# Logit spectra stored by frequency: long reads, short writes, a copied wrap and three more weight tiles

## The chip, the core and the metric

The program runs on one core of a Trainium2 chip. The metric is device time in microseconds (us). Engines are TensorE (PE, with its weight loads PEld), VectorE (DVE), ScalarE (ACT), GpSimd (POOL) and SyncE (SP), which here issues nearly all DMAs.

## What is computed

A spectral layer with soft thresholding, followed by a soft mixture of experts over all 8 x 2496 tokens:

```
X  = rfft(x, axis=1)                       # x: 8 x 2496 x 256
Yr = shrink(Xr @ w_r - Xi @ w_i + b_r)     # shrink: sign(y) * max(|y| - 0.01, 0)
Yi = shrink(Xr @ w_i + Xi @ w_r + b_i)
y  = irfft(Yr + 1j * Yi)                   # tokens, 19968 x 256
logits = y @ phi                           # 32 slots: 8 experts x 4
d = softmax over tokens;  slot_input = d.T @ y
slot_out[e] = relu(slot_input[e] @ w1[e]) @ w2[e]
out = softmax over slots (logits) @ slot_out
```

## The kernel before

**Transforms.** 2496 is 39 x 64, so a transform is one of length 39 (20 frequencies k are kept, K1) and one of length 64 (n, N2), joined by a transposition through DRAM. The 39-point matmuls work on three residues at once: R = 3 blocks of 39 tokens (or of 2 x 20 frequencies, real and imaginary, Q1 = 120 rows), each with G = 22 columns. 3 x 22 is 66, so the third block has 20 columns of its own and the first two of the signal once more.

**The main loop.** 40 steps, five groups of four frequencies for each of 8 batches. A step loads `ap` from the DRAM tile `adr` (line 387), transforms it (`px`), applies the weights (`pk`, `py`), shrinks on DVE and POOL (`ut`, `rt`), multiplies by phi (`pq`; its result `p_sb` is the logits' spectrum) and transposes `rt` into tiles `T`. Beside it the next batch's x is transformed (`pa`, `ast`) and written to `adr`.

**The logits of a batch** come from `p_sb` by an inverse transform of 32 columns (function `c_stages`, lines 604 to 706; `last_chain` from line 924 for batch 7). This is the place of the change:

1. `pg`: the 64-point matmul with the constant `sinv`. ACT copies it to `g_sb` (128 x 20 x 32). The rows are ordered n first, then real or imaginary (c).
2. `gd`, a DRAM tile `[64, 40, 32]`: `g_sb` is written to it in rows of 20 x 32 numbers, 2,560 B (line 619). Batch 7 writes three parts, as its frequencies get ready (line 936): 12, 4 and 4 of the 20.
3. `gp` (120 x 22 x 32): read from `gd` with four loads (lines 622 to 633, and 939 to 950), two of 40x22x32, one of 40x20x32 and one of 40x2x32 for the wrapped columns of the third block. Every contiguous piece has 32 numbers, 128 B.
4. ACT casts `gp` into `chpL`, DVE subtracts to get the rest `clpL`, and three matmuls per half give `pL` with the constant `m2`; `L` holds the logits. Batches 6 and 7 multiply `gp` itself, without the split.
5. From `L` come the running maximum (`mx`, `pm`, `mall`, `pb`), the exponentials `ee`, their forward transform (`pe`, `ea`, DRAM tile `ed`, read back as `eb`, then `pd`, `dd`) and the slot sums `pr` from `dd` and `T`.

**The tail.** After batch 7's `pr` come the experts (`psl`, `hps`, `po`) with 32 weight tiles of 512 KB, then the combine: 78 blocks of `pq`, copied by ACT and DVE and stored as `out`.

**What sets the order.** Every operation is a step of a generator with a due time; a heap runs them in that order, and the numbers in the table `PLAN` are the due times (the unit is a quarter of a step; TB = 166 is the end of the main loop). Each engine works through its list in that order and stops at the first thing that is not ready; so does SP's list of DMA issues (the helper `sp`, line 234; matmuls are recorded at line 240, the other engines at line 177). `PLAN["T_"]["wl"]` lists the 32 weight loads: due time, and where the tile lies: `r`, `a`, `x` and `T` are buffers that the main loop no longer needs (`x` and `T` in two halves of 256 KB), `t` and `h` are pools opened late. Pool `t` (tag `tw`) has `PLAN["nw"][1]` buffers of 4 KB per partition, shared by five tiles `T` of batch 6, weights, and the combine's `ct` and `chl`.

Of the kernel before, what the change touches and what calls it, by code (L numbers as in the profile page):

```python
# [11 lines left out]
F32 = mybir.dt.float32  # L12
# [37 lines left out]
def _constants():  # L50
    n1 = np.arange(N1)
    k1 = np.arange(K1)
    a39 = 2 * np.pi * (np.outer(n1, k1) % N1) / N1
    c39, s39 = np.cos(a39), np.sin(a39)
    s39[:, 0] = 0.0
    a64 = 2 * np.pi * (np.outer(np.arange(N2), np.arange(N2)) % N2) / N2
    q = np.outer(np.arange(N2), np.arange(N2)) % N2
    c64, s64 = np.cos(a64), np.sin(a64)
    c64[(q == 16) | (q == 48)] = 0.0
    s64[(q == 0) | (q == 32)] = 0.0  # L60

# [26 lines left out]
    smov = smov.reshape(128, K1 + 1, 64)
    smov = np.concatenate([smov[:, : KG + 1], smov[:, :1], smov[:, KG + 1 :]], axis=1).reshape(128, -1)
    sinv = suni[np.arange(128).reshape(2, N2).T.reshape(-1)].T  # L90
    sgn = np.ones((2, N2, K1))
    sgn[1] = sig.T
    sgn = sgn.reshape(128, K1)
    dsc = sgn * wk[None, :]

    ident = np.eye(128)
    dmask = np.tile(np.eye(32), (4, 4))
    f1a = f1.reshape(P1, R, 2, NGRP, KG).transpose(0, 3, 2, 4, 1).reshape(P1, Q1)
    f1 = f1.reshape(P1, R, 2 * K1).transpose(0, 2, 1).reshape(P1, Q1)
# [40 lines left out]
    "to": 0.7,  # L140
    "ws": [-29, -28.9, -28.8, 2],
    "late": {'6': {'cms': [19.75, 19.71, 860.75, 862, 864, 865], 'pd': [20.36, 20.37], 'pr': [31.55, 31.6, 31.65, 31.7, 31.75], 'pL': [5.4, 5.8], 'pm': 6.875, 'pb': 7.325, 'pe': [8.75, 9.75], 'pg': [0.875, 1.275], 'fr': {'sinv': 0, 'm2': 0, 'f1': 0, 'suni': 0}}, '5': {'pg': [1.1, 1.8], 'pL': [4.95, 5.75], 'pm': 6.8, 'pb': 7.15, 'pe': [9.2, 9.9], 'pd': [13.8, 14.8], 'pr': [15.0, 17.25, 19.5, 21.75, 24.0]}, '4': {'pr': [18.4, 20.49, 24.49, 28.49, 32.49]}},
    "T_": {'wl': [[-45, 'r'], [-44, 'r'], [-43, 'r'], [-31.0, 't'], [-30.7, 't'], [-29.4, 't'], [-27.6, 't'], [-27.8, 't'], [-11, 'a'], [-10.3, 'a'], [-9.6, 'a'], [-7.5, 'x'], [-6.4, 'x'], [1.11, 'x'], [1.07, 'h'], [1.08, 'h'], [1.09, 'h'], [1.1, 'h'], [1.11, 'h'], [13.55, 'h'], [13.1, 'h'], [13.6, 'h'], [13.6, 'h'], [13.61, 't'], [13.61, 't'], [13.61, 't'], [13.61, 't'], [13.61, 't'], [13.7, 'T'], [13.7, 'T'], [13.7, 'T'], [13.7, 'T']], 'cl': 16, 'cp': 46.5, 'ct': 46.6, 'du': [[-4.5, 0], [-2.4, 0], [1.2, 0]], 'd1': [5, 2, 4, 0, 0, 0], 'cm': [19.9, 19.91, 19.92, 25, 25.1, 25.2], 'cm7': [18, 20, 22, 23, 25, 27], 'ye': 0.2, 'te': [[5.6, 0.2], [5.5, 0.4]], 'pg': [-7, -3.25, -0.35], 'yt': 0.5, 'wr': -30.6, 'tp': [0, 0.9, 1.05, 0.5], 'tt': [[-0.4, 0.5, 0.6, 0.7, 0.8], [12, 12.1, 12.2, 12.3, 12.4]], 'z': 13.55, 'th': [0.1, 0.12], 'tl': [0.2, 0.25]},
    "f1": [1.5, 2.15],
    "kw": [[-40, 9]],
    "ap1": 1.85,
    "f0": 0.2,
    "nw": [3, 10, 9],
    "te": 'A',
    "tp": [0.5, 1.0, 1.9, 1.8],  # L150
    "tt": [2, 2.5],
# [29 lines left out]
def fourier_soft_moe_kernel(ctx: ExitStack, tc: tile.TileContext, t: dict, out: bass.AP):  # L181
    nc = tc.nc
# [3 lines left out]
    dr = ctx.enter_context(tc.tile_pool(name="dr", bufs=2, space=bass.MemoryType.DRAM))  # L186
# [30 lines left out]
    V, A, P = (_InOrder(tc, e) for e in (nc.vector, nc.scalar, nc.gpsimd))  # L217
# [15 lines left out]
    def sp(**kw):  # L233
        tc.keep_in_program_order(nc.sync.dma_start(**kw))  # L234
# [68 lines left out]
    ident, sgn, suni, sinv, dsc, dmask = (cols[k] for k in ("ident", "sgn", "suni", "sinv", "dsc", "dmask"))  # L303
    f1, m2 = cols["f1"][:P1], cols["m2"][:Q1]
# [273 lines left out]
    def halves(n, t0, times, out, const, fr, src, evac):  # L578
# [13 lines left out]
        for h in range(2):  # L592
# [8 lines left out]
            yield t0 + times[h] + 0.25  # L601
            evac(h, out[1](ps))

    def c_stages(b):
        ct_ = "ps"
        K_ = dict(PLAN, **PLAN["late"].get(str(b), {}))
        t0 = 20 * b + 20 + LAG
        yield t0 + PLAN["c0"]
        p_sb = psb[b]
        g_sb = wtile([128, K1, S], F32, "g_sb", f"g_sb{b}")  # L610
# [4 lines left out]
            lambda h, ps: A.copy(out=g_sb[:, h * 10 : h * 10 + 10, :].rearrange("p k s -> p (k s)"), in_=ps),  # L615
        )
        yield t0 + K_["pg"][1] + 0.35
        gd = dr.tile([N2, 2 * K1, S], F32, tag="gd", name=f"gd{b}")
        sp(out=gd.rearrange("n (c k) s -> (n c) k s", c=2), in_=g_sb)
        yield t0 + K_["pg"][1] + 0.9  # L620
        gp = wtile([Q1, G, S], F32, "gp", f"gp{b}")
        for r in range(R):
            ge = 22 if r < 2 else 20
            p0 = r * 2 * K1
            sp(
                out=gp[p0 : p0 + 2 * K1, :ge, :],
                in_=gd[22 * r : 22 * r + ge].rearrange("g k s -> k g s"),
            )
            if ge < G:
                sp(  # L630
                    out=gp[p0 : p0 + 2 * K1, ge:, :],
                    in_=gd[22 * r : 22 * r + G - ge].rearrange("g k s -> k g s"),
                )
# [51 lines left out]
        for c in range(2):  # L685
# [6 lines left out]
                out=dd[:, h * 10 : h * 10 + 10, :],  # L692
# [105 lines left out]
    TB = 4 * ns + LAG  # L798
# [125 lines left out]
    def last_chain():  # L924
        b = B - 1
        for (k0, k1), tk in zip(((0, 12), (12, 16), (16, 20)), T_["pg"]):
            ks = slice(k0, k1)
            n = (k1 - k0) * S
            yield TB + tk
            if k0 == 0:  # L930
                g_sb = wtile([128, K1, S], F32, "g7", f"g_sb{b}")
                gd = dr.tile([N2, 2 * K1, S], F32, tag="gd", name=f"gd{b}")
            ps = psum("pf", f"pg{b}_{k0}")
            mm(out=ps[:, :n], lhsT=sinv, rhs=psb[b][:, ks, :], start=True, stop=True)
            A.copy(out=g_sb[:, ks, :].rearrange("p k s -> p (k s)"), in_=ps[:, :n])
# [3 lines left out]
        for r in range(R):
            ge = 22 if r < 2 else 20  # L940
            p0 = r * 2 * K1
            sp(
                out=gp[p0 : p0 + 2 * K1, :ge, :],
                in_=gd[22 * r : 22 * r + ge].rearrange("g k s -> k g s"),
            )
            if ge < G:
                sp(
                    out=gp[p0 : p0 + 2 * K1, ge:, :],
                    in_=gd[22 * r : 22 * r + G - ge].rearrange("g k s -> k g s"),
                )  # L950
# [310 lines left out]
```

## Time and profile before

| | |
|---|---|
| runs | 579.31, 576.2, 579.02 us; median 579.02 |
| profiled execution | 575.19 us, of it 573.4 us span, 1.8 us around it |
| granted TensorE clock over the span | 0.971 |
| TensorE busy | 528.8 us, 92% |
| DMA queue of SP | 116.73 MB, 73.0% of 16 engines' span |
| packets under 512 B | 46,802 of 92,884 |

A row of a timeline is start and duration in us, engine, line, operation, tiles as out<-in, shape, count, and in brackets how long the engine stood still before it and what ended that. Rows of the chain are start, us, what. "SPq L234 gp<-gd" is the issue on SP, "DMA gp<-gd" the transfer from its issue to the landing. A matmul's row can overlap the next one's, since they are pipelined. Rows of windows give for each engine the busy time and the number of instructions, then the granted clock (1.00 is full), the mean busy share of 16 DMA engines (overlapping packets can bring it over 1) and GB/s.

### The profile page before, as it was taken

The page shows a single profiled execution, that of the slowest core. Times are in us where ns is not written, and L with a number is a line of the kernel's source. Part 1 is how long each engine was busy: PE and PEld are TensorE (multiplying, and loading weights), DVE is VectorE, ACT ScalarE, POOL GpSimd, SP SyncE. Part 2 cuts the span into 40 slices and gives each one's busy share as a digit, 9 for nine tenths or more (in the row PEclk, how much of TensorE's full clock was granted, in tenths as well). Part 3 has the DMA queues.
Part 4 walks back from the last instruction along what each step waited for, and adds up shares of the span by engine and source line. Part 5 has one row for each costly group of instructions (what it writes and reads, how often), then busy time and mean ns, then how long its engine had stood idle before and what let it go on. Part 6 is the DMA issues. An engine that isn't in the chain of part 4 may idle for free.

```text
span 573.4 us, 11788 instructions
## 1 busy us (share of the span) xinstructions
PE 528.8 (92%) x4358; PEld 447.4 (78%) x4358; DVE 419.3 (73%) x837; ACT 298.6 (52%) x650; POOL 281.0 (49%) x258
## 2 busy tenths in 40 slices
PE   8668999999999999999999999998899989799894
PEld 4357999989898879889988888897687767367673
DVE  0254988789979897989689977986776764247783
ACT  4334555667566656665665656553333333037662
POOL 0035778667676666658655865773445412000100
PEclk9887999999999999999999999998989999999897
DMA  8779878667776858775787577866624489969898
GB/s 241 235 259 241 198 162 175 156 171 178 205 176 178 173 154 204 170 180 156 177 196 187 151 179 185 238 184 193 164 80 102 121 199 298 369 218 363 330 374 352
DMA packets 92884, 118.55 MB, mean 207 GB/s; under 512 B 46802, under 2 KB 68624, under 8 KB 92828
## 3 DMA queue, kind: packets, MB, share of 16 engines
q1 hardware_dynamic: 92572, 116.73, 73.0%
q10 hardware_dynamic: 256, 1.08, 0.5%
q8 instruction: 34, 0.56, 0.4%
q14 instruction: 22, 0.18, 0.1%
HBM read 68.42 MB, written 49.38 MB: 205 GB/s over the span
## 4 chain that ended last, share of the span: by engine, by line
PE 65%; DMA 14%; DVE 12%; ACT 3%; issue 2%; SPq 2%; POOL 0%; ACTq 0%; DVEq 0%; POOLq 0%
PE py L240 15%; PE px L240 10%; PE pq L240 8%; PE pk L240 7%; PE pa L240 7%; PE pt L530 4%; DMA gp<-gd 3%; DMA gd<-g_sb 3%; PE pr L240 3%; DMA ap<-adr 2%; SPq L234 2%; PE pc L1065 2%; DMA eb<-ed 2%; DMA xr<-in_x 2%; DVE mx L177 1%
## 5 line engine op out<-in xcount | busy, mean ns | idle before, releaser
L177 POOL TENSOR_TENSOR rt<-ut,rt 128x512 f32<-128x512 f32 x79 | 111.7, 1414 | 26.5 <-DVE rt L177 22.0
L177 POOL TENSOR_TENSOR xsl<-xsm,xsh 128x256 fp32r<-128x256 f32 x77 | 59.4, 772 | 107.3 <-DVE xsh L177 72.5
L177 POOL TENSOR_TENSOR xl<-xr,xh 117x512 fp32r<-117x512 f32 x73 | 98.4, 1349 | 21.8 <-ACT xh L177 13.8
L240 PE MATMUL px<-smov,ap 128*128 128x128 f32 x640 | 86.8, 280 | 5.7 <-DMA ap<-adr 3.9
L240 PEld LDWEIGHTS px<-smov,ap 128*128 128x128 f32 x640 | 81.5, 195 | 11.6 <-issue 4.7
L177 ACT COPY ast<-pa 120x512 f32<-120x512 f32 x86 | 50.6, 588 | 69.7 <-PE pa L240 68.1
L177 ACT CAST xth<-px 128x512 fp32r<-128x512 f32 x80 | 46.9, 586 | 74.0 <-PE py L240 38.2
L177 DVE SCALAR_TENSOR_TENSOR ut<-py,pk,k 128x256 f32<-128x256 f32 x160 | 69.5, 475 | 16.7 <-PE py L240 12.4
L177 DVE TENSOR_TENSOR xtl<-px,xth 128x512 fp32r<-128x512 f32 x80 | 54.6, 683 | 24.7 <-ACT xsm L177 22.6
L240 PE MATMUL py<-xth,nwsh 128*128 128x256 f32 x160 | 54.0, 337 | 0.0
L177 DVE TENSOR_SCALAR rt<-ut 128x512 f32<-128x512 f32 x69 | 53.3, 772 | 0.5
L240 PE MATMUL pk<-xsh,w_rh 128*128 128x256 f32 x160 | 49.3, 308 | 2.0 <-DVE xsh L177 2.0
L530 PE MATMUL pt<-pk,rt 128*128 128x128 f32 x320 | 45.9, 273 | 0.9 <-DVE dd L177 0.6
L177 ACT COPY T<-pt 128x512 f32<-128x512 f32 x70 | 42.0, 599 | 9.0 <-PE pt L530 7.0
L240 PE MATMUL pk<-xsl,w_rh 128*128 128x256 f32 x160 | 46.2, 289 | 0.0
L240 PE MATMUL pk<-xsh,w_rl 128*128 128x256 f32 x160 | 46.1, 288 | 0.0
L240 PE MATMUL py<-xtl,wdh 128*128 128x256 f32 x160 | 45.3, 283 | 0.0
L240 PE MATMUL py<-xth,wdl 128*128 128x256 f32 x160 | 45.2, 283 | 0.0
L240 PE MATMUL py<-xth,nwsl 128*128 128x256 f32 x160 | 45.2, 283 | 0.0
L240 PE MATMUL py<-xth,wdh 128*128 128x256 f32 x160 | 45.2, 282 | 0.0
L240 PE MATMUL py<-xtl,nwsh 128*128 128x256 f32 x160 | 45.1, 282 | 0.0
L240 PE MATMUL pq<-rhs,ct 128*128 128x512 f32 x156 | 43.1, 416 | 0.3 <-DVE ost L177 0.3
(186 smaller groups left out, 1245.8 us busy)
## 6 DMA issues: line engine op xcount, KB each, us to landing
ap<-adr SPq DMA_DIRECT2D x76, 256.0 KB
out<-ost SPq DMA_DIRECT2D x37, 512.0 KB
xr<-in_x SPq DMA_DIRECT2D x35, 480.0 KB
adr<-ast SPq DMA_DIRECT2D x20, 720.0 KB
w<-in_moe_w SPq DMA_DIRECT2D x25, 512.0 KB
adr<-ast SPq DMA_DIRECT2D x8, 480.0 KB
w<-in_moe_w SPq DMA_DIRECT2D x14, 256.0 KB
x<-in_x SPq DMA_DIRECT2D x11, 240.0 KB
```

Of the source, the lines that this page charges most:

```text
L177: return lambda *a, **k: self.tc.keep_in_program_order(f(*a, **k))
L234: tc.keep_in_program_order(nc.sync.dma_start(**kw))
L240: tc.keep_in_program_order(nc.tensor.matmul(**kw))
L530: tc.keep_in_program_order(nc.tensor.transpose(out=out, in_=in_, identity=identity))
L1065: nc.tensor.transpose(out=pc[:, i * P1 : (i + 1) * P1], in_=chls[b][x][:, 2 * (r + i) : 2 * (r + i) + 2].rearrange("p g h s -> p (g h s)") ...
```

## The change

`gd` is laid out by frequency, `[2, 20, 64, 32]`. A row of one c and k is now 64 x 32 numbers, 8 KB in one piece.

- **Write**: two DMAs, one for each c, from 64 partitions each. In DRAM every piece is 128 B. Batch 7 writes its three parts with six DMAs. `sinv` is no longer permuted, so that the partitions of `g_sb` are c first.
- **Read**: three DMAs of 40 rows, each a contiguous stretch of 22 x 32 numbers (2,816 B), or 20 x 32 (2,560 B) for the third block. That block now lies in partitions 0 to 39 of `gp`, and the rows of `m2` are permuted to match.
- **Wrap**: the third block's last two columns are copied by ACT from the first block of `gp` itself, 40x64 numbers. It stands just before the first cast of `gp` (in batches 6 and 7 ahead of ACT's copies of `pL`).

```
+    def gd_write(gd, g_sb, k0, k1):
+        for c in range(2):
+            sp(out=gd[c, k0:k1].rearrange("k n s -> n k s"), in_=g_sb[c * N2 : c * N2 + N2, k0:k1, :])
+
+    def gp_read(gp, gd):
+        rows = gd.rearrange("c k n s -> (c k) (n s)")
+        q = 2 * K1
+        for r in range(2):
+            sp(
+                out=gp[q + q * r : q + q * r + q].rearrange("p g s -> p (g s)"),
+                in_=rows[:, r * G * S : (r + 1) * G * S],
+            )
+        sp(out=gp[:q, : G - 2, :].rearrange("p g s -> p (g s)"), in_=rows[:, 2 * G * S :])
+
+    def gp_wrap(gp):
+        A.copy(out=gp[: 2 * K1, G - 2 :, :], in_=gp[: 2 * K1, :2, :])
...
-        gd = dr.tile([N2, 2 * K1, S], F32, tag="gd", name=f"gd{b}")
-        sp(out=gd.rearrange("n (c k) s -> (n c) k s", c=2), in_=g_sb)
+        gd = dr.tile([2, K1, N2, S], F32, tag="gd", name=f"gd{b}")
+        gd_write(gd, g_sb, 0, K1)
...
-        for r in range(R):
-            ge = 22 if r < 2 else 20
...
+        gp_read(gp, gd)
         L = wtile([P1, G, S], F32, "L", f"L{b}")
+        yield t0 + K_["pL"][0] - PLAN["cl"][0] - 0.01
+        gp_wrap(gp)
...
-    "nw": [3, 10, 9],
+    "nw": [3, 13, 9],
...
-    nc = _bacc.Bacc("TRN2", target_bir_lowering=False, num_devices=1)
+    nc = _bacc.Bacc("TRN2", target_bir_lowering=False, num_devices=1, dynamic_dma_scratch_size=1024)
```

The same three steps replace write and read in `last_chain`. The two constants change by one line each:

```
-    m2 = m2.reshape(Q1, P1)
+    m2 = m2[[2, 0, 1]].reshape(Q1, P1)
...
-    sinv = suni[np.arange(128).reshape(2, N2).T.reshape(-1)].T
+    sinv = suni.T
```

The build sets the DMA scratch to 1 KB per partition, and pool `t` has 13 buffers instead of 10. In the table of weight loads three `t` entries are new, at -24, -22 and -20 before TB. The two `x` entries at -7.5 and -6.4 move to 1.12 and 1.13 behind it. Of the late entries (13.55 and after), one more is `x`, and three that used `T` are gone.

On SP in batch 0, from the write of `gd` on (numbers in names are buffers), before:

```order
L234 DMA gd_1290<-g_sb_1178 128x640
L234 DMA ap_4_1315<-adr_182 64x4x256 x2
L234 DMA gp_1326<-gd_1290 40x22x32 x2
L234 DMA gp_1326<-gd_1290 40x20x32
L234 DMA gp_1326<-gd_1290 40x2x32
```

and now:

```order
L234 DMA gd_1290<-g_sb_1178 64x20x32 x2
L234 DMA ap_4_1316<-adr_182 64x4x256 x2
L234 DMA gp_1327<-gd_1290 40x704 x2
L234 DMA gp_1327<-gd_1290 40x640
```

The write became two issues, the read three, and `ap` still stands between them. So it is in batches 1 to 4; in batch 5 an `adr` write stands there, in batch 6 nothing, with a new weight load just ahead of the write.

On ACT in batch 0, at the cast of `gp`, before:

```order
L177 COPY ast_0_1395<-pa_0_1396 120x512
L177 CAST chpL_0_1405<-gp_1326 120x352
L177 CAST chpL_1_1421<-gp_1326 120x352
L177 CAST xth_4_0_1438<-px_4_0_1415 128x512
```

and now:

```order
L177 COPY ast_0_1395<-pa_0_1396 120x512
L177 COPY gp_1327<-gp_1327 40x64
L177 CAST chpL_0_1406<-gp_1327 120x352
L177 CAST chpL_1_1422<-gp_1327 120x352
L177 CAST xth_4_0_1439<-px_4_0_1416 128x512
```

The copy of the wrapped columns is new, ahead of both casts; the rest of ACT's list is the same, and so are the lists of the other compute engines but for the buffers that hold the weights.

On SP at the end of the main loop, batch 7's `gd` and `gp` and the weights `w` (tile number first) around them, before:

```order
L234 DMA w11_1_6426<-in_moe_w1 128x512
L234 DMA gd7_6432<-g_sb7_6431 128x384
L234 DMA w12_0_6439<-in_moe_w1 128x512
L234 DMA w12_1_6440<-in_moe_w1 128x512
L234 DMA gd7_6432<-g_sb7_6431 128x128 x2
L234 DMA gp7_6540<-gd7_6432 40x22x32 x2
L234 DMA gp7_6540<-gd7_6432 40x20x32
L234 DMA gp7_6540<-gd7_6432 40x2x32
L234 DMA w13_6547<-in_moe_w1 128x1024
...
L234 DMA ed7_6608<-ea7_6595 120x704
L234 DMA w19_6705<-in_moe_w2 128x1024
L234 DMA eb7_6707<-ed7_6608 64x20x32 x2
```

and now:

```order
L234 DMA gd7_6441<-g_sb7_6440 64x12x32 x2
L234 DMA gd7_6441<-g_sb7_6440 64x4x32 x4
L234 DMA gp7_6548<-gd7_6441 40x704 x2
L234 DMA gp7_6548<-gd7_6441 40x640
L234 DMA w14_6554<-in_moe_w1 128x1024
...
L234 DMA w20_1_6569<-in_moe_w2 128x512
L234 DMA ed7_6620<-ea7_6607 120x704
L234 DMA eb7_6717<-ed7_6620 64x20x32 x2
```

Weights w11 and w12 no longer stand between the writes. Between `gp` and `ed` there are now seven tiles (w14 to w20), before six (w13 to w18); the one between `ed` and `eb` is gone.

More of the change, by code (lines that the diff above doesn't have):

```diff
@@ L142 @@
     "late": {'6': {'cms': [19.75, 19.71, 860.75, 862, 864, 865], 'pd': [20.36, 20.37], 'pr': [31.55, 31.6, 31.65, 31.7, 31.75], 'pL': [5.4, 5.8], 'pm': 6.875, 'pb': 7.325, 'pe': [8.75, 9.75], 'pg': [0.875, 1.275], 'fr': {'sinv': 0, 'm2': 0, 'f1': 0, 'suni': 0}}, '5': {'pg': [1.1, 1.8], 'pL': [4.95, 5.75], 'pm': 6.8, 'pb': 7.15, 'pe': [9.2, 9.9], 'pd': [13.8, 14.8], 'pr': [15.0, 17.25, 19.5, 21.75, 24.0]}, '4': {'pr': [18.4, 20.49, 24.49, 28.49, 32.49]}},
-    "T_": {'wl': [[-45, 'r'], [-44, 'r'], [-43, 'r'], [-31.0, 't'], [-30.7, 't'], [-29.4, 't'], [-27.6, 't'], [-27.8, 't'], [-11, 'a'], [-10.3, 'a'], [-9.6, 'a'], [-7.5, 'x'], [-6.4, 'x'], [1.11, 'x'], [1.07, 'h'], [1.08, 'h'], [1.09, 'h'], [1.1, 'h'], [1.11, 'h'], [13.55, 'h'], [13.1, 'h'], [13.6, 'h'], [13.6, 'h'], [13.61, 't'], [13.61, 't'], [13.61, 't'], [13.61, 't'], [13.61, 't'], [13.7, 'T'], [13.7, 'T'], [13.7, 'T'], [13.7, 'T']], 'cl': 16, 'cp': 46.5, 'ct': 46.6, 'du': [[-4.5, 0], [-2.4, 0], [1.2, 0]], 'd1': [5, 2, 4, 0, 0, 0], 'cm': [19.9, 19.91, 19.92, 25, 25.1, 25.2], 'cm7': [18, 20, 22, 23, 25, 27], 'ye': 0.2, 'te': [[5.6, 0.2], [5.5, 0.4]], 'pg': [-7, -3.25, -0.35], 'yt': 0.5, 'wr': -30.6, 'tp': [0, 0.9, 1.05, 0.5], 'tt': [[-0.4, 0.5, 0.6, 0.7, 0.8], [12, 12.1, 12.2, 12.3, 12.4]], 'z': 13.55, 'th': [0.1, 0.12], 'tl': [0.2, 0.25]},
+    "T_": {'wl': [[-45, 'r'], [-44, 'r'], [-43, 'r'], [-31.0, 't'], [-30.7, 't'], [-29.4, 't'], [-27.8, 't'], [-27.6, 't'], [-24, 't'], [-22, 't'], [-20, 't'], [-11, 'a'], [-10.3, 'a'], [-9.6, 'a'], [1.07, 'h'], [1.08, 'h'], [1.09, 'h'], [1.1, 'h'], [1.11, 'h'], [1.12, 'x'], [1.13, 'x'], [13.55, 'x'], [13.6, 'h'], [13.6, 'h'], [13.6, 'h'], [13.6, 'h'], [13.61, 't'], [13.61, 't'], [13.61, 't'], [13.61, 't'], [13.61, 't'], [13.7, 'T']], 'cl': 16, 'cp': 46.5, 'ct': 46.6, 'du': [[-4.5, 0], [-2.4, 0], [1.2, 0]], 'd1': [5, 2, 4, 0, 0, 0], 'cm': [19.9, 19.91, 19.92, 25, 25.1, 25.2], 'cm7': [18, 20, 22, 23, 25, 27], 'ye': 0.2, 'te': [[5.6, 0.2], [5.5, 0.4]], 'pg': [-7, -3.25, -0.35], 'yt': 0.5, 'wr': -30.6, 'tp': [0, 0.9, 1.05, 0.5], 'tt': [[-0.4, 0.5, 0.6, 0.7, 0.8], [12, 12.1, 12.2, 12.3, 12.4]], 'z': 13.55, 'th': [0.1, 0.12], 'tl': [0.2, 0.25]},
     "f1": [1.5, 2.15],
@@ L617, in c_stages @@
         yield t0 + K_["pg"][1] + 0.35
-        gd = dr.tile([N2, 2 * K1, S], F32, tag="gd", name=f"gd{b}")
-        sp(out=gd.rearrange("n (c k) s -> (n c) k s", c=2), in_=g_sb)
+        gd = dr.tile([2, K1, N2, S], F32, tag="gd", name=f"gd{b}")
+        gd_write(gd, g_sb, 0, K1)
         yield t0 + K_["pg"][1] + 0.9
         gp = wtile([Q1, G, S], F32, "gp", f"gp{b}")
-        for r in range(R):
-            ge = 22 if r < 2 else 20
[L624 to L633, printed above, removed]
+        gp_read(gp, gd)
         L = wtile([P1, G, S], F32, "L", f"L{b}")
+        yield t0 + K_["pL"][0] - PLAN["cl"][0] - 0.01
+        gp_wrap(gp)
         yield from halves(
@@ L931, in last_chain @@
                 g_sb = wtile([128, K1, S], F32, "g7", f"g_sb{b}")
-                gd = dr.tile([N2, 2 * K1, S], F32, tag="gd", name=f"gd{b}")
+                gd = dr.tile([2, K1, N2, S], F32, tag="gd", name=f"gd{b}")
             ps = psum("pf", f"pg{b}_{k0}")
@@ L935, in last_chain @@
             A.copy(out=g_sb[:, ks, :].rearrange("p k s -> p (k s)"), in_=ps[:, :n])
-            sp(out=gd.rearrange("n (c k) s -> (n c) k s", c=2)[:, ks, :], in_=g_sb[:, ks, :])
+            gd_write(gd, g_sb, k0, k1)
         yield TB + 1
         gp = wtile([Q1, G, S], F32, "gp", f"gp{b}")
[L939 to L950, printed above, removed]
+        gp_read(gp, gd)
         L = wtile([P1, G, S], F32, "L", f"L{b}")
         mx = wtile([P1, 4, S], F32, "mx", f"mx{b}")
+        yield TB + 6.9
+        gp_wrap(gp)
         yield TB + 7
```

## The prediction, made before the result was known

> **What bounds the kernel now.** I read the page first: the busy shares and the chain that ended last.
>
> ```profile
> span 573.4 us, 11788 instructions
> PE 528.8 (92%) x4358; PEld 447.4 (78%) x4358; DVE 419.3 (73%) x837; ACT 298.6 (52%) x650; POOL 281.0 (49%) x258
> ...
> PE 65%; DMA 14%; DVE 12%; ACT 3%; issue 2%; SPq 2%; POOL 0%; ACTq 0%; DVEq 0%; POOLq 0%
> PE py L240 15%; PE px L240 10%; PE pq L240 8%; PE pk L240 7%; PE pa L240 7%; PE pt L530 4%; DMA gp<-gd 3%; DMA gd<-g_sb 3%; PE pr L240 3%; DMA ap<-adr 2%; SPq L234 2%; PE pc L1065 2%; DMA eb<-ed 2%; DMA xr<-in_x 2%; DVE mx L177 1%
> ```
>
> TensorE carries the program, but the edited transfer is on the chain with 6% of it (gd and gp), some 35 us. That is no gain yet: TensorE works beside most of it. What can be won is the time in which TensorE stands still behind it, so the second view is the waits of TensorE from 60 to 500 us (total us, times, longest).
>
> ```profile
> PE pd L240 <- DMA eb<-ed: 3.1, 1, 3.1
> PE pL L240 <- ACT chpL L177: 2.4, 1, 2.4
> PE pL L240 <- DMA gp<-gd: 2.4, 1, 2.4
> PE pm L648 <- DVE mx L177: 2.2, 5, 0.8
> PE px L240 <- DMA ap<-adr: 0.8, 2, 0.6
> ```
>
> Four places hang on gp. pL waits once for ACT's cast of gp (batch 5) and once for gp itself (batch 7). pm waits five times, in batches 0 to 4, for DVE, which had waited for the same cast. px waits in batch 6 for ap, whose loads stand behind gp's on SP. Everything below is the price of these four, and of eb in batch 7.
>
> **The transfer, priced.** In the chain, batch 5 (start, us, what):
>
> ```profile
> 380.90 2.24 DMA gd<-g_sb
> 383.15 0.29 SPq L234
> 383.49 2.12 SPq L234
> 385.66 4.34 DMA gp<-gd
> 390.10 0.49 ACT chpL L177
> ```
>
> Batch 7, where nothing is left to do beside it:
>
> ```profile
> 465.53 2.80 DMA gd<-g_sb
> 468.41 0.30 SPq L234
> 468.76 0.57 SPq L234
> 469.38 3.87 DMA gp<-gd
> 473.38 1.41 PE pL L240 x4
> ...
> 484.62 5.61 DMA eb<-ed
> ```
>
> Write and read are in series. From the first gp issue to the landing it takes 6.85 us in batch 5 (383.15 to 390.00) and 4.84 us in batch 7. The next view gives stretches by windows (PE, PEld, DVE, ACT, POOL busy, clock, DMA share, GB/s). In the first only gp's packets move, in the second eb's, in the third rows of 4 KB, in the fourth mostly gd's rows of 2,560 B.
>
> ```profile
> 469.50:472.00 2.50, 1.52 (x14) 1.28 (x12) 1.88 (x3) 1.36 (x3) 0.00 (x0) 1.00 0.80 124
> 485.50:487.00 1.50, 1.50 (x16) 1.50 (x15) 1.24 (x2) 0.93 (x3) 1.50 (x4) 1.00 1.14 183
> 474.00:478.00 4.00, 3.43 (x24) 2.80 (x23) 2.54 (x8) 0.90 (x2) 0.00 (x0) 1.00 1.00 383
> 437.00:438.00 1.00, 1.00 (x12) 1.00 (x11) 0.94 (x2) 0.23 (x1) 0.65 (x1) 1.00 0.73 278
> ```
>
> A 128 B piece costs 128 B / (124 GB/s / 16 / 0.80) = 13 ns of a DMA engine. gp's 2,640 pieces (338 KB) need 338/124 = 2.7 us. After the change the 128 B pieces are on the write: 2,560 of them, 64x20x32 per load, the same shape as eb's reads, which run at 183 GB/s, so 328/183 = 1.8 us. The old write needs 328/278 = 1.2 us. The new read is 120 rows of 2,560 or 2,816 B: 0.9 us at 383 GB/s, 2.7 us at worst as now; I take 1.3.
>
> The trace has no write of 128 B pieces. Bounds: 13 ns (as read) and 26 ns (each written as if read first); I take 13, since it is the row of the same size, and keep 26 as a rival.
>
> Now the issues, from SP's timeline (start, us, what, count):
>
> ```profile
> 412.50 1.24 SPq L234 DMA_DIRECT2D ap<-adr  x2
> ...
> 436.45 0.34 SPq L234 DMA_DIRECT2D gd<-g_sb  x1
> 439.78 2.67 SPq L234 DMA_DIRECT2D gp<-gd  x4
> 442.54 1.25 SPq L234 DMA_DIRECT2D ap<-adr  x2
> ...
> 463.38 0.89 SPq L234 DMA_DIRECT2D w<-in_moe_w  x2
> ...
> 468.41 2.85 SPq L234 DMA_DIRECT2D gp<-gd  x4
> 471.43 3.47 SPq L234 DMA_DIRECT2D w<-in_moe_w  x7
> ...
> 481.21 0.38 SPq L234 DMA_DIRECT2D w<-in_moe_w  x1
> 484.00 1.39 SPq L234 DMA_DIRECT2D eb<-ed  x2
> ```
>
> Four gp issues hold SP for 2.7 to 2.9 us. An issue of long rows takes 0.34 (gd), so three take about 1.0. Two gd issues take what eb's two take, 1.4 instead of 0.34, though the data of the first start meanwhile: I charge 0.3 to the path and 0.6 to the data (1.8 less 1.2), so **the write lands 0.9 us later** (bounds 0.3 and 2.7). Nearest to the new read is the 2.24 us in which gd's long rows landed in batch 5: third issue at 0.7, landing at 2.9 from the first issue, against 4.84. **The read lands 1.9 us sooner** (bounds 0.5 and 2.2).
>
> The copy of two columns on ACT: 40x64 elements. Its nearest row is 128 elements per partition:
>
> ```profile
> 470.23 0.29 ACT L177 COPY zrow<-dd 1x128 f32<-1x128 f32 x1
> ```
>
> I take 0.2 ahead of chpL in batches 0 to 5. It waits for the third load, as chpL behind it must anyway; queued behind both on ACT are the next xth and xsm, as now. In batch 7 only the second half of pL reads the copied columns, so it lies beside the first pL.
>
> **The four places.** *Batches 0 to 4*: the same three steps, here batch 0 in the chain:
>
> ```profile
> 107.23 3.98 DMA gd<-g_sb
> 112.45 3.77 DMA gp<-gd
> 117.32 1.60 DVE clpL L177
> ```
>
> The write shares the engines with the adr write ahead of it and ap follows it, so less comes off: 1.9 less 0.9 less 0.2 is 0.8 at best. Only the 2.2 us of pm's waits can be recovered, and DVE is crowded. I take 0.9 over the five (bounds 2.2 and -5.5, the second under the rival).
>
> *Batch 5*: gp's second issue stood 2.12 us behind the 720 KB adr write. Write +0.9, so gp starts at 384.0; the read takes 2.9 and some 1.1 of that queue; landing 388.0, copy 0.2, against chpL at 390.10: 1.9 earlier, of 2.4 waited; I take 1.7. TensorE's clock also fell after this wait:
>
> ```profile
> 390.60:392.60 2.00, 1.97 (x8) 1.88 (x9) 1.81 (x4) 1.75 (x5) 0.00 (x0) 0.50 1.06 294
> 392.60:394.60 2.00, 2.00 (x14) 1.98 (x14) 1.81 (x6) 0.45 (x1) 1.41 (x2) 0.76 0.22 86
> 473.40:476.00 2.60, 2.51 (x14) 1.89 (x15) 1.49 (x4) 0.90 (x2) 0.00 (x0) 1.00 1.00 362
> ```
>
> Granted 0.50 and 0.76 over 4 us cost 1.0 and 0.5 us of work; after the equal wait of batch 7 it stayed 1.00, so it is not certain to follow. With 0.6 us left of the wait I expect most of it back: 1.0. Sum 2.7 (bounds 0 and 3.9).
>
> [...]
>
> *Batch 6*: ap's loads stand behind gp's on SP; its issues end 1.7 us sooner and start up to 0.9 later, which removes the 0.6 us of px: 0.5. The copy waits for a load that is there by then.
>
> *Batch 7*: the three parts of the write are 64 KB at the end, so they grow little, and the four half tiles of weights (463.38 and the pair before) no longer stand ahead of them. I let the landing stay at 468.3 (1 us either way). The read: 468.3 + 2.9 = 471.2 against 473.25. TensorE has other work until 2.4 us before 473.38, so no more than that can come off; 2.2 (bounds 0.5 and 2.4).
>
> By the order on SP, shown with the change, no weight stands between the writes any more, nor between ed and eb. That tile (512 KB, 1.4 us at 383 GB/s) was ahead of eb, whose landing took 5.61 us. But seven tiles instead of six now stand ahead of ed; they start 2.2 us earlier, which is 840 KB at that rate, against 524 KB more. I take 0.4 (bounds -2.2 and 1.4). Batch 7: 2.6.
>
> **The rest is nothing.** The three further weight tiles load between the ap issue at 412.50 and gd at 436.45, behind ap and ahead of gd on SP: 1.6 MB in 24 us, hidden by the matmuls of two steps; a tile that ran into gd there would cost 1.4 us. After eb there are eleven tiles to load instead of twelve. The output phase is unchanged.
>
> **Sum**: 0.9 + 2.7 + 0.5 + 2.6 = 6.7 us. The profiled execution took 575.19 us (span 573.4), so it would take 568.5. It is the fastest seen: the three runs have a median of 579.02, and from that I predict 572.3.
>
> **Rivals.** *A, slower: the small pieces cost double when written.* Place: gd in batches 0 to 4. At 26 ns the write needs 1.8 us more, so chpL comes 1.0 to 1.1 us later than before (0.8 at best, less 1.8), five times, and pm's waits grow by it: +5.5. Batch 5 keeps nothing, batch 6 nothing, batch 7 2.2: +3.3, or 582.3. Between -6.7 at 13 ns and +3.3 at 26 ns it turns to a loss at about 22 ns a piece. For it: nothing in the trace writes so small. Against it: reads of this size show no surcharge. Chance 0.17. [...]
>
> *B, no change: another transfer ends last.* If ed must wait for the seventh tile (3.7 MB at 383 GB/s from 471.2 ends at 480.8, just where ed was issued), batch 7 gives nothing; if batch 5 keeps its slow clock, it gives 1.0. Left: 0.9 + 1.0 + 0.5 = 2.4, or 576.6. For it: the DMA share of 1.00 from 474 to 478. Against it: TensorE's 2.4 us wait for gp goes in any case. Chance 0.17.
>
> **How the numbers follow.** Forecast 0.66, B 0.17, A 0.17. About 0.5% (2.9 us) is what a measurement can tell from no change: faster 0.66; within it 0.20 (B and the mild part of A); slower 0.14. All best ends together are 10.5 us, so 568.5, and 1 us for the spread of runs gives 567.5; upward the range takes in B and the milder part of A, to 581.
>
> **What would show it.** Right: three gp issues of 0.3 us; gp landing some 3 us after the first; pL's two waits under 0.7 us; clock 1.00 at 390; chpL in batches 0 to 4 not later than before. Wrong: gd's landing over 2.5 us later, pm's waits growing, or eb landing no sooner in the program although pL does.

## The result, and the profile after

| | before | after |
|---|---|---|
| median, us | 577.61 (4 runs, 575.93 to 579.31) | 583.62 (4 runs, 580.85 to 585.09) |
| profiled execution, us | 575.19 | 583.56 |
| its span, us | 573.4 | 581.6 |

The ratio after to before is 1.0116, 95% interval 1.0068 to 1.0165: slower by 1.2%, some 6.7 us. The two medians are 6.0 us apart; every ratio here is of runs in the usual, faster state of the chip, the medians are of all runs. The forecast was 6.7 us faster, and the range ended at 581.0.

The page after, first its span, TensorE's row and the chain that ended last:

```profile
span 581.6 us, 11769 instructions
...
PE 531.1 (91%) x4358; PEld 448.1 (77%) x4358; DVE 413.8 (71%) x837; ACT 298.6 (51%) x658; POOL 279.5 (48%) x258
...
PE 67%; DMA 14%; DVE 8%; ACT 5%; SPq 2%; issue 2%; POOL 0%; ACTq 0%
PE py L240 15%; PE px L240 10%; PE pq L240 8%; PE pk L240 7%; PE pa L240 7%; DMA gd<-g_sb 4%; DMA gp<-gd 4%; PE pt L530 4%; PE pr L240 3%; SPq L234 2%; PE pc L1064 2%; PE pL L240 2%; DMA xr<-in_x 2%; PE pe L240 2%; DMA ap<-adr 1%
```

The same 4,358 matmuls take 531.1 us instead of 528.8; gd and gp moved up the chain, from 6% to 8% of it. TensorE's waits from 60 to 510 us (total us, times, longest):

```profile
PE pL L240 <- DMA gp<-gd: 4.8, 2, 2.7
PE pL L240 <- ACT chpL L177: 4.0, 2, 3.0
PE pd L240 <- DMA eb<-ed: 3.2, 1, 3.2
...
PE pm L656 <- ACT xth L177: 1.5, 3, 0.5
...
PE pm L656 <- DVE mx L177: 0.9, 2, 0.5
```

The wait of pL for gp and for its cast was to fall from 4.8 us (2.4 and 2.4) to under 1.4. It rose to 8.8. pm waits 2.4 us in all, as against 2.2 before, but now mostly for ACT. eb's wait, to shrink by 0.4, stayed (3.1 before, 3.2 now). SP's timeline shows where it comes from (start, us, what, count): the write of batch 5, an `adr` write behind it and the read, then batch 6 and batch 7.

```profile
385.87 1.42 SPq L234 DMA_DIRECT2D gd<-g_sb  x2
387.35 0.98 SPq L234 DMA_DIRECT2D adr<-ast  x1
391.21 1.12 SPq L234 DMA_DIRECT2D gp<-gd  x3
...
441.19 1.40 SPq L234 DMA_DIRECT2D gd<-g_sb  x2
446.68 1.06 SPq L234 DMA_DIRECT2D gp<-gd  x3
...
470.13 4.86 SPq L234 DMA_DIRECT2D gd<-g_sb  x6
477.00 1.05 SPq L234 DMA_DIRECT2D gp<-gd  x3
```

The read is issued when the write has landed. In batch 5 that is 5.34 us after the first gd issue (385.87 to 391.21; before 380.90 to 383.15, 2.25), in batch 6 5.49 us (before 436.45 to 439.78, 3.33). The write lands 3.1 and 2.2 us later, not 0.9. In batches 0 to 4, where it was slow before too (4.0 to 4.5 us), it lands 0.3 to 2.1 us later, in three of the five 0.84 to 0.87. In batch 7 six issues hold SP for 4.86 us. The three read issues do cost the 1.0 us that was forecast.

The chain in batch 5 (start, us, what):

```profile
386.51 4.65 DMA gd<-g_sb
...
392.00 3.57 DMA gp<-gd
...
395.74 0.49 ACT chpL L177
```

and in batch 7, with eb at its end:

```profile
472.43 0.57 SPq L234
473.05 0.62 SPq L234
473.71 0.61 SPq L234
474.37 2.58 DMA gd<-g_sb
...
477.73 3.46 DMA gp<-gd
...
492.86 5.50 DMA eb<-ed
```

From the last gp issue the read still takes 3.57 and 3.46 us, with long rows, where it took 4.34 and 3.87 with 2,640 pieces. From the first issue it is 4.19 us in batch 7 (477.00 to 481.19) against 4.84 before: 0.65 us saved, not 1.9. By the packets in the trace (2,816 and 2,560 B), its rows pass from 477.91 to 480.86; the last of them share the engines with a weight tile that SP issues right behind (rows of 4 KB, from 479.28 on).

Windows after (busy times, clock, DMA share, GB/s): the first two hold the write of batch 6, which has the DMA engines nearly to itself, the third gp's long rows, the fourth TensorE behind the wait of batch 5.

```profile
443.00:444.50 1.50, 1.50 (x16) 1.50 (x15) 1.05 (x3) 0.97 (x3) 1.05 (x1) 1.00 0.89 138
444.50:446.00 1.50, 1.50 (x15) 1.44 (x13) 0.88 (x3) 0.00 (x0) 0.73 (x1) 1.00 0.22 31
478.00:479.00 1.00, 0.58 (x6) 0.34 (x4) 0.82 (x2) 0.66 (x2) 0.00 (x0) 1.00 0.57 205
398.00:400.00 2.00, 2.00 (x8) 1.93 (x9) 1.97 (x7) 0.45 (x1) 1.18 (x2) 0.50 0.02 6
```

A written piece of 128 B costs 128 B / (138 GB/s / 16 / 0.89) = 13.2 ns of an engine, the price that was forecast, and not 26: no doubled price of a piece, although the write as a whole lands late. What differs from eb's reads of the same shape is how well the engines are filled: share 0.89 against 1.14, 138 GB/s against 183, and then a tail of 1.5 us at 31 GB/s. The long rows of gp run at 205 GB/s, with a share of 0.57, not at the 383 GB/s of the weights.

Where did the time go? The next table gives, from the starts of TensorE's instructions in the traces, the us from the last `pg` to the first `pL` of a batch. In it lie the copy of `g_sb`, write, read and casts; in batches 0 to 4 TensorE's other work fills much of it. The kernels e1 to e10 are those of the experiments.

| | batches 0 to 4, sum | 5 | 6 | 7 | all |
|---|---|---|---|---|---|
| before | 60.91 | 10.53 | 8.90 | 8.46 | 88.80 |
| after | 62.83 | 11.20 | 10.91 | 8.84 | 93.78 |
| e1_weights | 60.91 | 11.07 | 8.66 | 6.69 | 87.33 |
| e2_layout | 61.75 | 10.81 | 9.52 | 9.54 | 91.62 |
| e3_one_write | 63.32 | 11.54 | 9.91 | 6.66 | 91.43 |
| e4_halves | 61.04 | 9.42 | 8.77 | 7.40 | 86.63 |
| e5_old_halves | 60.91 | 10.15 | 8.66 | 6.70 | 86.42 |
| e6_pieces | 62.91 | 11.65 | 9.88 | 7.23 | 91.67 |
| e7_two_reads | 74.18 | 14.12 | 14.20 | 11.33 | 113.83 |
| e8_one_read | 61.32 | 9.62 | 9.37 | 8.34 | 88.65 |
| e9_rows_first | 60.96 | 10.01 | 10.00 | 7.03 | 88.00 |
| e10_wrap_copy | 60.98 | 10.20 | 8.66 | 6.86 | 86.70 |

After is 5.0 us above before. The two profiled executions differ by 8.4 us; 1.7 of it stands ahead of the first edited DMA (`pg` of batch 0 starts at 107.77 instead of 106.06), and that start scatters from 105.0 to 110.1 over the traces of this study without regard to the edit. The last 1.7 us have no single place. The clock does not account for them: between 100 and 520 us both traces have it at 0.50 for 10.2 us in all, though in other places.

### The profile page after: what moved, and what is told of

Its sections match the earlier page's. It is cut to its first block, busy times and chain, and to the rows that moved or that the text cites. A ratio compares the mean times of both kernels' runs of the same rounds, so it can differ in the third digit from the quotient of the medians.

```text
span 581.6 us, 11769 instructions
## 1 busy us (share of the span) xinstructions
PE 531.1 (91%) x4358; PEld 448.1 (77%) x4358; DVE 413.8 (71%) x837; ACT 298.6 (51%) x658; POOL 279.5 (48%) x258
## 4 chain that ended last, share of the span: by engine, by line
PE 67%; DMA 14%; DVE 8%; ACT 5%; SPq 2%; issue 2%; POOL 0%; ACTq 0%
PE py L240 15%; PE px L240 10%; PE pq L240 8%; PE pk L240 7%; PE pa L240 7%; DMA gd<-g_sb 4%; DMA gp<-gd 4%; PE pt L530 4%; PE pr L240 3%; SPq L234 2%; PE pc L1064 2%; PE pL L240 2%; DMA xr<-in_x 2%; PE pe L240 2%; DMA ap<-adr 1%
## 5 line engine op out<-in xcount | busy, mean ns | idle before, releaser
L177 POOL TENSOR_TENSOR xl<-xr,xh 117x512 fp32r<-117x512 f32 x73 | 97.1, 1330 | 23.1 <-ACT xh L177 15.1
```

The lines of the kernel that those rows point to most:

```text
L177: return lambda *a, **k: self.tc.keep_in_program_order(f(*a, **k))
```

## The experiments

The theory after the result, **W**: the write in 128 B pieces is on the path and costs more than the read gives back. Rivals: **T**, the moved weight loads; **S**, the 1 KB scratch, at the start of the program; **I**, the number of DMA issues on SP. All ratios below are to the kernel before, run beside them on the same chip.

### e1_weights and e2_layout: the two halves of the change

e1 is before with the weight table, the 13 buffers and the scratch; e2 is after without these.

```
e1:
-    "T_": {'wl': [... [-27.6, 't'], [-27.8, 't'], [-11, 'a'], ...
+    "T_": {'wl': [... [-27.8, 't'], [-27.6, 't'], [-24, 't'], [-22, 't'], [-20, 't'], [-11, 'a'], ...
-    "nw": [3, 10, 9],
+    "nw": [3, 13, 9],
+    ... dynamic_dma_scratch_size=1024
e2: after, with these lines as before
```

> The old layout of gd with the new weight table, 13 tile buffers and the 1 KB scratch: the transfer stays as before. Theory W (the loss is the write in 128 B pieces): the time of before, 577.6, within 2 us; gd lands 2.2 us after its issue in batch 5 as before; in batch 7 the write is free of weights, so up to 1 us may come off. Rival T (the moved weight loads and the tail cost it): 581 or more, with later landings of eb in batch 7. Rival S (the scratch size delays the start, where the trace after was 1.7 us late before any gd): the px wait near 43 us grows from 3.1 to 4.0, about 579.

> The new layout alone, with the weight table, 10 buffers and scratch of before. Theory W: the time of after, 583.6, within 2 us; gd lands over 5 us after its first issue in batches 5 and 6; batch 7 is worse than in after by up to 1 us, since four half weight tiles stand between the six writes. Rival T: 578. Rival S: 1.7 us less than after, about 582, with the px wait near 43 us back at 3.1.

e1: 574.66 us (10 runs), ratio 0.9979 [0.9954, 1.0004]. e2: 586.26 us (6 runs), ratio 1.0207 [1.0160, 1.0255]. T and S fall: alone, weights and scratch cost nothing. The layout carries the whole loss. Alone it even costs more than the whole change (2.1% against 1.2%), and more than theory W expected; the traces place 0.7 us of the difference in batch 7 (9.54 against 8.84), where weight tiles stand between the six writes, and the rest is open. In e1's trace batch 7 goes from `pg` to `pL` in 6.69 us instead of 8.46; no weight tile stands between the three writes there. After, with the same weights and six issues for the writes, takes 8.84.

### e3_one_write: one issue for real and imaginary

`gd` becomes `[20, 2, 64, 32]`, so that 128 partitions form one stride and one DMA writes them. Pieces and read stay.

```
-        for c in range(2):
-            sp(out=gd[c, k0:k1].rearrange("k n s -> n k s"), in_=g_sb[c * N2 : c * N2 + N2, k0:k1, :])
+        sp(out=gd[k0:k1].rearrange("k c n s -> (c n) k s"), in_=g_sb[:, k0:k1, :])
```

> As after, but gd is [20, 2, 64, 32] and each write one DMA of 128 partitions, so the 128 B pieces are the same 2,560 and only the second issue of 0.6 us goes (three of them in batch 7). If the number of issues is a main part of the loss: gd's landing 0.6 us sooner in each batch, batch 7's pL 1.3 to 1.9 sooner, 583.6 less 3 to 4, about 580. If only the pieces and their landing count: within 1 us of after, 583.

580.30 us (8 runs), ratio 1.0065 [1.0028, 1.0102], some 3 us under after; the two intervals overlap a little. SP's timeline, batches 5 and 6:

```profile
388.04 0.40 SPq L234 DMA_DIRECT2D gd<-g_sb  x1
...
391.90 2.37 SPq L234 DMA_DIRECT2D gp<-gd  x3
...
443.36 0.38 SPq L234 DMA_DIRECT2D gd<-g_sb  x1
448.35 1.05 SPq L234 DMA_DIRECT2D gp<-gd  x3
```

The write lands after 3.86 and 4.99 us, against 5.34 and 5.49 with two issues. So issues are a part of the loss, and not all of it. From `pg` to `pL` the gain shows in batches 6 and 7 (1.0 and 2.2 us by the table). In batch 5 it is lost again: the three gp issues take 2.37 us instead of 1.12, behind the `adr` write that stands ahead of them.

### e4_halves: start the first half of the write early

As e3, but in batches 0 to 6 each half of `g_sb` is written when ACT has copied it.

```
+        def g_out(h, ps):
+            A.copy(out=g_sb[:, h * 10 : h * 10 + 10, :].rearrange("p k s -> p (k s)"), in_=ps)
+            gd_write(gd, g_sb, h * 10, h * 10 + 10)
...
-        gd_write(gd, g_sb, 0, K1)
```

> As the one-write kernel, but each half of g_sb (10 of the 20 frequencies) is written as soon as ACT has copied it, in batches 0 to 6. The data time of the first half then lies before the second half is ready. Theory W (data time of the written pieces on the path): the landing after the last issue falls from about 4.7 to 3.3 us, pL's waits in batches 1, 5 and 6 fall by 1 us each, some 576 to 578. If the landing is a fixed price of such a write and not its data: as the one-write kernel, within 1 us.

574.52 us (10 runs), ratio 0.9968 [0.9933, 1.0002]: 5.8 us under e3, and level with before. TensorE's waits for gp, in e3 and then in e4:

```profile
PE pL L240 <- ACT chpL L177: 4.7, 3, 3.4
...
PE pL L240 <- DMA gp<-gd: 1.7, 2, 1.1
```

```profile
PE pL L240 <- issue: 1.3, 1, 1.3
PE pL L240 <- ACT chpL L177: 1.3, 1, 1.3
```

With half of the pieces beside the second `pg`, the wait for the cast is down to 1.3 us, and in e4's trace the clock stays at 1.00 behind the wait of batch 5 (1.27 us long), where e3's falls to 0.50:

```profile
390.50:394.00 3.50, 3.50 (x24) 3.04 (x25) 3.29 (x9) 2.12 (x7) 0.94 (x2) 1.00 0.57 177
```

The same bytes in the same pieces cost nothing that shows when half of them are hidden.

### e5_old_halves: is halving a gain of its own?

e1 with the old rows of `gd`, written in halves (1,280 B each).

```
+            sp(out=gd.rearrange("n (c k) s -> (n c) k s", c=2)[:, hs, :], in_=g_sb[:, hs, :])
...
-        sp(out=gd.rearrange("n (c k) s -> (n c) k s", c=2), in_=g_sb)
```

> The layout of before with the new weight table (as e1_weights), and each half of g_sb written to gd as soon as ACT has copied it, in batches 0 to 6. Theory W (the time goes into writing 128 B pieces; the early start of the first half only hides that): rows of 1,280 B need little hiding, so some 0 to 2 us less than e1_weights, 573 to 575, ratio 0.993 to 0.998, gd landing about 2.5 us after the last issue. Rival H (halving is a gain of its own, whatever the layout): as much less as e4_halves gained on e3_one_write, 5.8 us, so 569, ratio 0.989.

574.09 us (12 runs), ratio 0.9952 [0.9922, 0.9982]. That is 0.3% under e1, whose interval overlaps it; the 5.8 us of e4 over e3 do not come back. Rival H falls: halving pays where there are small pieces to hide.

### e6_pieces: small pieces, and nothing else

e1 with each row of 32 numbers padded to 64 in DRAM. One issue, 128 partitions, the old four reads; only the write falls into 2,560 pieces of 128 B.

```
-        gd = dr.tile([N2, 2 * K1, S], F32, tag="gd", name=f"gd{b}")
+        gd = dr.tile([N2, 2 * K1, 2 * S], F32, tag="gd", name=f"gd{b}")[:, :, :S]
```

> As e1_weights (old layout, one DMA of 128 partitions, the same four reads), but each row of 32 numbers of gd is padded to 64 in DRAM, so that the write goes in 2,560 pieces of 128 B and nothing else changes. Theory W: the write of batch 5 lands 4.5 us or more after its issue instead of 2.2, and the time is 3 to 7 us over e1_weights, 578 to 582, ratio 1.003 to 1.010. Rival I (only the number of issues on SP matters, pieces are free): lands as before, 574.7, ratio 0.998.

582.41 us (11 runs), ratio 1.0106 [1.0069, 1.0143]: 7.3 us over e1 (1.0106 less 0.9979 of 575.7). The pieces alone cost as much as after loses as a whole. SP's timeline of e1, batches 5 and 6:

```profile
382.33 0.35 SPq L234 DMA_DIRECT2D gd<-g_sb  x1
...
384.59 4.67 SPq L234 DMA_DIRECT2D gp<-gd  x4
...
437.32 0.33 SPq L234 DMA_DIRECT2D gd<-g_sb  x1
439.68 2.68 SPq L234 DMA_DIRECT2D gp<-gd  x4
```

and of e6:

```profile
384.55 0.55 SPq L234 DMA_DIRECT2D gd<-g_sb  x1
...
388.58 4.74 SPq L234 DMA_DIRECT2D gp<-gd  x4
...
441.31 0.55 SPq L234 DMA_DIRECT2D gd<-g_sb  x1
445.36 2.66 SPq L234 DMA_DIRECT2D gp<-gd  x4
```

The write lands after 4.03 and 4.05 us instead of 2.26 and 2.36: pieces cost 1.7 us with one issue (a landing after 4.5 us or more had been expected). By the packets in the two traces, 1.2 us of it in batch 6 is data: e1's 128 rows pass from 438.15 to 439.29, e6's 2,560 pieces from 442.52 to 444.85. In e6's window of that write a piece has the same price again, 128 / (147 / 16 / 0.90) = 12.5 ns:

```profile
443.30:444.50 1.20, 1.20 (x13) 1.20 (x12) 0.97 (x2) 0.71 (x2) 0.87 (x1) 1.00 0.90 147
```

The padding also spaces the rows that are read: from the first gp issue to the cast it takes 5.6 us on average in batches 0 to 4, against 5.2 in e1, and in batch 5 6.28 against 7.48. So a small part of the loss in batches 0 to 4 may be the read's.

Rival I in its pure form (pieces are free) falls. The table shows what 1.7 us a batch do: 2.0 us over batches 0 to 4, 0.6 in 5, 1.2 in 6, 0.5 in 7, 4.3 in all against e1. The other 3 us of the 7.3 lie outside that stretch. The two traces place 1.8 us of them right behind batch 6's `pL`, here the rows of px in e1 and then in e6:

```profile
447.33 1.13 PE L240 MATMUL px<-smov,ap 128*128 128x128 f32 x8
```

```profile
453.21 2.04 PE L240 MATMUL px<-smov,ap 128*128 128x128 f32 x8 [0.62 <-DMA ap<-adr]
```

px waits 0.62 us for ap, whose loads stand behind gp's on SP, and takes 2.04 us instead of 1.13, since e6's clock is at 0.50 from 452.9 to 456.3 (after's too, from 452.5 to 455.9), where e1's and before's stay at 1.00. One trace of each does not tell how often the clock falls there.

### e7_two_reads, e9_rows_first, e8_one_read: the read

Why did the long rows save 0.65 us and not 1.9? On e4, two loads instead of three: blocks 0 and 1 as one load of 80 rows.

```
+        sp(
+            out=gp[q:].rearrange("p g s -> p (g s)"),
+            in_=rows[:, : 2 * G * S].rearrange("a (r x) -> r a x", r=2),
+        )
```

> As e4_halves, but the two loads of 40 long rows are one load of 80 rows, so that the read is two DMAs. Theory R (the read is slow because a load of 40 rows keeps only some of the 16 engines busy and each issue costs 0.35 us): landing 3.0 to 3.6 us after the first issue instead of 4.2 to 4.4, time 573, ratio 0.994. Rival F (a fixed delay of the DMA makes up the landing): landing 4.0, time as e4_halves, ratio 0.997.

609.56 us (6 runs), ratio 1.0566 [1.0511, 1.0620]. Neither theory foresaw 35 us more. The chain in batch 7:

```profile
497.98 7.99 DMA gp<-gd
```

A new theory, **E**, an estimate from this trace: how many packets of a load move at a time follows from its first dimension, here 2. The 80 packets take 152 ns each, and they pass in 6.2 us (498.71 to 504.89), as 40 of them one behind the other would (6.1 us): two at a time on average. A row takes 2,816 B / (205 GB/s / 16 / 0.57) = 125 ns by the window of after, so 40 take 5.0 us with nothing beside them; and the loads of 40 rows in after, with a share of 0.57, kept some nine of 16 engines busy. e9 is the same load with the dimensions the other way round:

```
-            in_=rows[:, : 2 * G * S].rearrange("a (r x) -> r a x", r=2),
+            in_=rows[:, : 2 * G * S].rearrange("a (r x) -> a r x", r=2),
```

with the rows of `m2` permuted to match. In e8 a row of `gd` has 66 columns, so that all 120 stretches lie at one stride and a single load reads them. The two added columns hold zeros in place of the wrapped ones, nothing of the output comes from them, and the copy on ACT is gone. The write needs two DMAs again.

```
+        sp(out=gp.rearrange("p g s -> p (g s)"), in_=gd.rearrange("k c (r g) s -> (k c r) (g s)", r=R))
```

For e9, E put the landing at 3.6 to 4.2 us and the time at 574 us; for e8, the landing at 2.8 to 3.3 us after the issue and the time at 573.

> As e7_two_reads, the same two loads with the same bytes and pieces, but the load of 80 rows has its dimensions the other way round, first 40 frequencies and then 2 blocks, with the rows of m2 permuted to match. [...] Rival P (a load of 80 rows is slow for its number of rows or partitions, whatever their order): as e7_two_reads, 609, ratio 1.057.

> As e4_halves, but a row of gd has 66 columns in DRAM, so that its 120 stretches of 2,816 B lie one behind the other and gp is read by one load of 120 rows. The two added columns hold zeros (nothing of the output comes from them), the copy of the wrapped columns is gone, and the write is two DMAs per half again, since real and imaginary rows no longer form one stride. [...] Rival F (the fixed parts of a load make up the time): landing 3.8 or more, ratio 0.997 or worse.

e9: 578.52 us (12 runs), ratio 1.0051 [1.0022, 1.0080]. e8: 576.60 us (12 runs), ratio 1.0013 [0.9984, 1.0042]. The reads of batch 7 in the chain, e9 and then e8:

```profile
470.31 3.56 DMA gp<-gd
```

```profile
471.44 3.62 DMA gp<-gdz
```

and windows of e8 in that read, before the first row of a weight tile at 473.61:

```profile
472.25:473.00 0.75, 0.61 (x6) 0.37 (x4) 0.57 (x2) 0.65 (x2) 0.00 (x0) 1.00 0.72 109
473.00:473.50 0.50, 0.00 (x0) 0.00 (x0) 0.50 (x1) 0.04 (x1) 0.00 (x0) 1.00 0.80 315
```

E holds in the step from e7 to e9: only the order of the dimensions differs, and 31 us are gone; from the last issue to the landing it takes 3.56 us instead of 7.99. Why the order counts, no run shows. E holds half in e8: with 120 rows in one load the rate reaches 315 GB/s instead of 205, and by the packets the rows pass in 1.8 us (472.40 to 474.21) instead of 2.95 in after (477.91 to 480.86). But the landing comes 3.62 us after the issue, between E's 2.8 to 3.3 and the 3.8 of rival F: 0.96 us pass before the first row, with the issue, and 0.85 after the last. These 1.8 us are not data, as F has it.

And neither is faster than e4. In e8 the six writes of batch 7 are back, and `pg` to `pL` takes 8.34 us there against 7.40 in e4. e9, expected at 574, took 4 us more than e4; the table's measure puts 1.4 us of that between `pg` and `pL` (88.00 in all). In the rest the clock has a part: e9's trace has it at 0.50 for 3.4 us from 416.4, from 447.1 and from 491.5, and e4's at no time between 100 and 530. Whether e9's other runs have that too, no trace shows.

### e10_wrap_copy: the copy alone

e5 with three loads of gp in the old pieces, and the wrapped columns copied by ACT as in the change.

```
+    def gp_wrap(gp):
+        A.copy(out=gp[: 2 * K1, G - 2 :, :], in_=gp[: 2 * K1, :2, :])
...
+        for r in range(3):
+            ge = G if r < 2 else G - 2
+            p0 = (r + 1) % 3 * q
+            sp(out=gp[p0 : p0 + q, :ge, :], in_=gd[G * r : G * r + ge].rearrange("g k s -> k g s"))
```

> As e5_old_halves (gd written in rows of 1,280 B, in halves), with the one part of the change that touches neither layout nor piece: three loads of gp instead of four, and the wrapped columns copied by ACT. Theory W (only the small pieces of the write cost): one issue of 0.5 us less on the path of batches 5 and 7 and the copy of 0.2 us more in batches 0 to 5, so 0.3 to 1 us less than e5_old_halves, 573.5, ratio 0.994. Rival C (the copy, which waits for the last load and stands ahead of the casts on ACT, is itself a cost of the change): 1 to 3 us more, 576, ratio 0.999 or more.

574.38 us (12 runs), ratio 0.9962 [0.9932, 0.9991], not to be told from e5. Rival C falls: the copy costs nothing that shows, and the issue that it saves gains nothing that shows. (The wrapped columns, copied now and loaded before, are the third block's own first two; the section on the kernel before calls them the first two of the signal.)

The fastest version is thus e5: the old layout with halved writes and the new weight table, 0.48% under before, with an interval from 0.18 to 0.78%. e1, e4 and e10 lie within 0.3% of it and are not told apart from it.

## Why the prediction was wrong

| term of the sum (gain, us) | forecast | `pg` to `pL`, before less after |
|---|---|---|
| batches 0 to 4 | 0.9 | -1.9 |
| batch 5, transfer | 1.7 | -0.7 |
| batch 5, clock | 1.0 | none |
| batch 6 | 0.5 | -2.0 |
| batch 7, transfer | 2.2 | -0.4 |
| batch 7, eb | 0.4 | -0.1 (wait for eb) |

**"The write lands 0.9 us later": the step that failed.** The price of a piece was right (13.2 ns). The error is in turning it into a time. I divided the bytes by 183 GB/s, the rate of eb's reads at a share of 1.14, and got 0.6 us more of data. The price itself gives more: 2,560 pieces of 13 ns on 16 full engines are 2.1 us, not 1.8. The written pieces ran at 138 GB/s, their engines less filled, and left a tail. e6 measures this part by itself: the write lands 1.7 us later, 1.2 of it data. The second issue was charged with 0.3 us, as the data of the first would start meanwhile; with it the write of after lands 3.1 us later in batch 5, above the upper bound of 2.7, and 2.2 in batch 6. A row of the same size and shape, but of the other direction, was taken as the nearest. Whether the direction mattered is not shown: the other read of such pieces in the prediction, gp's, ran at 124 GB/s with a share of 0.80, and by it the data would have taken 2.6 us (328/124), where e6's took 2.3.

**"The read lands 1.9 us sooner": mis-sized, 0.65 in batch 7.** The landing after the last issue was put at 2.24 us, that of gd's rows in batch 5. Nearer was gp's own row in batch 7, 3.87 us after its last issue. Less the 1.4 us of data that the long rows were to save (2.7 less 1.3), 2.5 remains; 3.46 was measured. The loads of forty rows did not fill sixteen engines (a share of 0.57 and 205 GB/s, so 1.6 us for 338 KB), and the third load's rows passed beside a weight tile, so that all rows took 2.95 us and not the 1.3 of the sum; no run keeps that tile away. The lower bound, 0.5, was right for batch 7. Only in batch 5, where the read had stood behind the `adr` write, is the saving large: 6.85 us from the first issue to the landing before, 4.36 now (391.21 to 395.57), for which the forecast had 4.0.

In batches 0 to 4 the read came later in all but batch 3: its last row passes 4.98, 6.06, 5.21, 3.74 and 4.66 us after the first gp issue, against 4.39, 4.19, 3.87, 5.07 and 4.23 before. With the later write, the cast starts 1.0 to 2.6 us later behind the copy of `g_sb`, where the prediction took 0.8 us off at best and named a later chpL as a sign of being wrong. Why long rows are slower there, no run shows.

With the measured sizes the signs follow. Batch 5: write 3.1 later, read 2.5 shorter, 0.6 lost; the table has 0.7. Batch 6: write 2.2 later, and from the first gp issue to `pL` it is 4.50 us (446.68 to 451.18) against 4.65 (439.78 to 444.43); 2.0 lost, as in the table.

**Issues and copy: right.** Three read issues took 1.05 to 1.12 us. With the copy between them, the cast of batch 5 starts 0.17 us after the landing (392.00 + 3.57, and 395.74), and e10 finds no cost in it.

**The clock of batch 5**: its 1.0 us hung on a wait under 0.7 us. The wait grew to 3.0, and the clock fell to 0.50 as before. e4 comes nearest to the case that was forecast: its wait is 1.27 us, and the clock stays at 1.00. So the recovery is there to be had, but not by a rule of the wait's length alone: in e10 the clock stays at 1.00 behind a wait of 2.04 us, and in after it falls behind one of 2.09 in batch 6.

**Batch 7: "I let the landing stay", wrong twice.** Without weights between the writes the old layout gains 1.8 us there (e1, 8.46 to 6.69). After, with six issues of some 0.6 us, 4.86 with the pauses between them, lost that and 0.4 more: the last issue starts at 474.37, 1.3 us after its data are in `g_sb` (473.07). I had priced the parts by their bytes ("64 KB at the end") and not by their issues.

**The three weight tiles and the scratch are nothing: right**, shown by e1.

**The rivals.** Rival A gave 582.3 us, and 583.62 was measured, but not by its mechanism: no doubled price, and the loss is not all in pm's waits for DVE, which fell from 2.2 to 0.9 us. The waits stand at pL instead. That it came near the time is luck. The "no surcharge" of small reads held against 26 ns only: a read piece costs 13 ns, where 128 B at the rate of the weights (383 GB/s, share 1.00) take 5.3. Rival B's point, that eb would end no sooner, held; it decided nothing.

Open: why written pieces leave the engines less filled (share 0.89) than eb's reads (1.14), and fuller than gp's (0.80). The runs show that they do, not the cause.

## What to carry to other kernels

A layout that trades short reads for short writes is not an even trade even where a packet costs the same (13 ns either way here, and e6's write lands 1.7 us later): price the write by a write, from its issue to its landing, with every issue that it needs. In e8 1.5 us of a 3.6 us read (3.62 less 1.81 and 0.35) were neither data nor issue; so look first at what can start earlier, as the first half of the write did. And put a long dimension first, not one of 2 (609.56 us in e7, 578.52 in e9).

## What the runs showed of the hardware

- A read with a load whose first dimension is 2 landed 7.99 us after its last issue, the same bytes with 40 first 3.56 us after it. 120 rows in one load moved at 315 GB/s, three loads of 40 at 205.
- A written piece of 128 B costs the 13 ns of a read one, yet 328 KB of them land 1.7 us later than in rows of 2,560 B (e6 against e1).
- An issue of the write takes 0.32 to 0.38 us in long rows (before, e1), 0.36 to 0.40 in pieces in e3, 0.55 to 0.57 in e6 before batch 7 and 0.57 to 0.66 in after's batch 7. The number of pieces hardly matters for a write alone: batch 7's last ones have 256 each and take 0.57 to 0.62, e6's whole write has 2,560 and takes 0.55. But the second of after's two writes takes 0.77 to 1.16.
- The clock fell to 0.50 behind a wait of 2.38 us in batch 5 of the kernel before, and stayed at 1.00 behind one of 2.37 us in its batch 7.
